# A gate in one step from PSUM, softmax sums spread in f16 halves, wider conversion and a new instruction order

## The chip, the cores and the metric

The kernel runs on one core of a Trainium2 chip. The metric is device time of one execution, in microseconds. In the text TensorE is the matmul engine (PE in the rows, PEld for its weight loads), VectorE is DVE, ScalarE is ACT, GpSimd is POOL, and SP is the engine that only issues transfers.

## What is computed

Attention for 4 batches of 12 heads (448 positions of 64), then a gated layer that mixes positions, then a feed-forward layer with a layer norm, all in f32 accuracy:

```python
q_n, k_n = rmsnorm(q, g_q), rmsnorm(k, g_k)
attn = softmax(q_n @ k_n.T / sqrt(64))              # sum + 1e-9 in the divisor
x = heads side by side of (attn @ v)                # 4 x 448 x 768
h = maximum(x @ w_in, 0)                            # 768 -> 1024
u, v = h[..., :512], h[..., 512:]
v_n = (v - mean(v)) / sqrt(var(v) + 1e-6)
v_s = einsum('ts,bsd->btd', w_spatial, v_n) + b_spatial[None, :, None]
x = (u * v_s) @ w_out                               # 512 -> 768
xn = layernorm(x) * g_ln
out = x + maximum(xn @ w_ch1, 0) @ w_ch2            # 768 -> 3072 -> 768
```

All weights but `w_spatial` come as 64-bit floats.

## The kernel before

f32 accuracy on f16 matmuls comes from splitting each operand into a high and a low f16 part and adding three products (high·high, high·low, low·high). Operands are scaled by powers of two first. `sum_scale` (L70) makes such a scale: VectorE casts partial maxima, TensorE adds them over the partitions by a product with ones (L83, tiles `ssb` and `pssc`), VectorE shifts exponents (L85 to L90, `sst`, `wsc`).

Attention goes in 24 pairs of heads. `att_slot` (L341) makes the scores of a pair in four groups (`s_mm`, L240, two score banks `ps_s`), their maximum (L251, VectorE), the exponential (L256, ScalarE), splits it into f16 halves (L275 ScalarE, L276 VectorE) and multiplies by v (L300; the first six pairs in f32, L293). `av_scale` (L304) spreads the reciprocals of the softmax sums, 7 per partition, over the positions: VectorE puts them on a diagonal `dg` (L311), TensorE multiplies it by a block of ones (L314, f32), ScalarE copies the result to `rb` (L316), which `av_out` multiplies in (L327).

The gated layer, `moe1` (L543), runs once per batch. It makes v and its norm (L563 to L577, `vn16`), u (L584, relu and scale on ScalarE at L587), then the spatial product for each of four quarters f of 128 columns (L597, tile `pss`, two banks). What follows it is:

```python
nc.vector.scalar_tensor_tensor(vs, ps[:, :S], isp[:, 0:1], c.bsp, op0=ALU.mult, op1=ALU.add)
nc.gpsimd.tensor_tensor(u[:, f], u[:, f], vs, op=ALU.mult)
nc.vector.tensor_reduce(gm[:, f:f + 1], u[:, f], axis=AX.X, op=ALU.max, apply_absolute_value=True)
```

and after the fourth quarter `sum_scale` over the four maxima, the f16 halves of the gated values (L611 ScalarE, L612 VectorE, `g16`) and the output product (L625, L635), which goes to DRAM (`x2d`). The layer of batches 0 to 2 lies beside attention, that of batch 3 beside the layer norms of the first half (batches 0 and 1).

`load_weight` (L395) turns 64-bit weights into f32 with three integer operations on VectorE per row block (L415 to L417). For the 12 blocks of `w_ch1` a transfer brings three row blocks of 256 columns each, for `w_ch2` one of 768.

The feed-forward layer runs in 12 blocks of 256 hidden columns and two halves of 896 positions: `ffn1` (L704, seven products of nine matmuls with sums between them on VectorE, L711 to L736, tiles `ps1x` to `ps1w` in three banks) and `ffn2` (L755, twelve matmuls per 128 positions, tile `ps2` with two buffers, added to the result by VectorE at L759). `prep_w1` and `prep_w2` load and split the weights of a block, `layernorm` (L645) makes the input.

The order on every engine is set at the end by `issue_order` (L1019): a planner runs forwards and backwards over the whole program with costs written in the code, and the table `SHAKES` says with which random shifts (seed, size, passes) the priorities are moved between runs. Every engine works through its queue in the order so found. SP's queue holds the transfers.

## Time and profile before

| | |
|---|---|
| time, median of 3 runs | 1175.62 us (1172.11 to 1179.37) |
| profiled execution, its own time | 1177.03 us |
| its span, first to last instruction | 1175.2 us |
| mean granted clock of TensorE | 0.967 |
| TensorE busy | 1049.7 us, 89% |
| VectorE busy | 958.4 us, 82% |
| ScalarE busy | 592.0 us, 50% |
| GpSimd busy | 295.6 us, 25% |

A profile is one execution. Busy time of an engine is the time in which at least one of its instructions ran. A row of a timeline has the start, the duration, the line of the kernel and the tile written and read; what stands in brackets is the idle time before it and what ended it. The chain of waits is followed back from the last instruction, at each step to what released it.

### The profile page before, as it was taken

The page shows a single profiled execution, that of the slowest core. Times are in us where ns is not written, and L with a number is a line of the kernel's source. Part 1 is how long each engine was busy: PE and PEld are TensorE (multiplying, and loading weights), DVE is VectorE, ACT ScalarE, POOL GpSimd, SP SyncE. Part 2 cuts the span into 40 slices and gives each one's busy share as a digit, 9 for nine tenths or more (in the row PEclk, how much of TensorE's full clock was granted, in tenths as well). Part 3 has the DMA queues.
Part 4 walks back from the last instruction along what each step waited for, and adds up shares of the span by engine and source line. Part 5 has one row for each costly group of instructions (what it writes and reads, how often), then busy time and mean ns, then how long its engine had stood idle before and what let it go on. Part 6 is the DMA issues. An engine that isn't in the chain of part 4 may idle for free.

```text
span 1175.2 us, 16716 instructions
## 1 busy us (share of the span) xinstructions
PE 1049.7 (89%) x6173; PEld 549.9 (47%) x6173; DVE 958.4 (82%) x1724; ACT 592.0 (50%) x1128; POOL 295.6 (25%) x209
## 2 busy tenths in 40 slices
PE   0679879989969998957789999999999999999998
PEld 0234324444435444423345555555555555555554
DVE  6798888869895987877988897888979788787755
ACT  2789878668776964646434334232423423243310
POOL 3454453726945520322001011010101101010100
PEclk9999879989989999978899999999999999999999
DMA  7978889899999996767773212112121211211013
GB/s 244 240 201 221 192 169 201 168 219 202 183 199 193 183 161 182 160 147 218 177 161 106 81 54 81 54 55 81 54 72 37 81 54 55 81 54 55 1 41 148
DMA packets 248913, 154.70 MB, mean 132 GB/s; under 512 B 209600, under 2 KB 226048, under 8 KB 248832
## 3 DMA queue, kind: packets, MB, share of 16 engines
q1 hardware_dynamic: 244448, 142.63, 51.4%
q10 hardware_dynamic: 4384, 11.01, 2.8%
q8 instruction: 48, 0.79, 0.3%
q14 instruction: 33, 0.27, 0.1%
HBM read 86.63 MB, written 11.01 MB: 83 GB/s over the span
## 4 chain that ended last, share of the span: by engine, by line
PE 48%; DVE 4%; issue 0%; DVEq 0%
PE ps L755 25%; PE ps1w L704 6%; PE ps1z L704 6%; PE ps1x L704 6%; PE ps1y L704 3%; DVE x L669 1%; DVE x L759 1%; DVE w1v L509 0%; DVE r_f L417 0%; DVE lst L656 0%; DVE r_f L416 0%; DVE h L717 0%; DVE lv L677 0%; DVE lv L679 0%; DVE lv L678 0%
## 5 line engine op out<-in xcount | busy, mean ns | idle before, releaser
L755 PE MATMUL ps<-w,h 128*128 128x384 f16 x2016 | 356.9, 327 | 7.8 <-DVE x L759 3.8
L755 PEld LDWEIGHTS <-h 128*128 128x128 f16 x2016 | 197.1, 98 | 150.7 <-issue 10.3
L759 DVE SCALAR_TENSOR_TENSOR x<-ps,wio,x 128x768 f32<-128x768 f32 x168 | 170.2, 1014 | 61.8 <-PE ps L755 60.3
L704 PEld LDWEIGHTS <-w1v 128*128 128x128 f16 x1512 | 147.7, 98 | 136.7 <-issue 8.9
L500 POOL TENSOR_TENSOR sums<-r_f 128x384 f32<-128x384 f32 x12 | 13.1, 1089 | 464.2 <-ACT r_f L497 464.2
L240 PE MATMUL ps_s<-hT 128*64 128x448 f16 x672 | 99.5, 386 | 32.6 <-ACT pexp L256 27.9
L256 ACT ACTIVATE pexp<-ps_s,nb 128x448 f32<-128x448 f32 x168 | 107.0, 650 | 33.1 <-DVE nb L251 32.1
L251 DVE TENSOR_REDUCE nb<-ps_s 128x2 f32<-128x896 f32 x96 | 91.2, 966 | 24.6 <-PE ps_s L240 24.1
L704 PE MATMUL ps1w<-xnT,w1v 128*128 128x448 f16 x432 | 92.7, 359 | 5.4 <-DVE rst_x L537 3.4
L704 PE MATMUL ps1x<-xnT,w1v 128*128 128x448 f16 x432 | 91.0, 352 | 0.0
L704 PE MATMUL ps1z<-xnT,w1v 128*128 128x448 f16 x432 | 90.6, 352 | 0.0
L276 DVE SCALAR_TENSOR_TENSOR p<-pexp,p 128x896 f16<-128x896 f32 x72 | 79.3, 1104 | 12.9 <-ACT p L275 12.7
L240 PEld LDWEIGHTS <-hT 128*64 128x64 f16 x672 | 39.8, 115 | 89.8 <-issue 56.9
L275 ACT ACTIVATE p<-pexp 128x896 f16<-128x896 f32 x72 | 61.6, 862 | 1.6 <-DMA pT<-p 0.7
L185 POOL TENSOR_TENSOR rs<-ss,mhalf 128x28 f32<-128x28 f32 (+1 forms) x12 | 58.4, 4868 | 13.1 <-DVE ss L182 8.5
L563 PE MATMUL psv<-w_v,xT 128*128 128x512 f16 (+1 forms) x360 | 61.2, 341 | 0.0
L584 PE MATMUL psu<-xT,w_u 128*128 128x448 f16 x288 | 59.8, 353 | 1.2 <-ACT vr L567 1.0
L203 POOL TENSOR_TENSOR qk<-raw,qk 128x896 f16<-128x896 f32 x23 | 45.5, 1979 | 55.8 <-ACT qk L202 54.0
L417 DVE SCALAR_TENSOR_TENSOR r_f<-r_w,r_f 128x256 int32<-128x256 int32 (+1 forms) x96 | 56.1, 584 | 1.3
L625 PE MATMUL pso<-w_o,g 128*128 128x384 f16 x288 | 53.0, 334 | 2.2 <-ACT g L611 1.9
L416 DVE SCALAR_TENSOR_TENSOR r_f<-r_w,r_f 128x256 int32<-128x256 int32 (+1 forms) x96 | 53.4, 556 | 1.5
L724 ACT ACTIVATE tp<-ps1x 128x448 f32<-128x448 f32 x24 | 13.0, 542 | 75.7 <-PE ps1x L704 75.4
(214 smaller groups left out, 1677.5 us busy)
## 6 DMA issues: line engine op xcount, KB each, us to landing
r_w<-in_moe_w_ch_dram SPq DMA_DIRECT2D x48, 768.0 KB, 4.4
raw<-in_q_dram SPq DMA_DIRECT2D x24, 224.0 KB, 3.4
raw<-in_k_dram SPq DMA_DIRECT2D x24, 224.0 KB, 3.5
vraw<-in_v_dram SPq DMA_DIRECT2D x24, 224.0 KB, 3.8
vpre<-in_v_dram SPq DMA_DIRECT2D x12, 448.0 KB, 4.6
...
```

Of the source, the lines that this page charges most:

```text
L185: nc.gpsimd.tensor_tensor(rs, ss, c.mhalf[:, 0:14 * m], op=ALU.pow)
L240: nc.tensor.matmul(ps[hd * 64:hd * 64 + 64, :S], p.hT[:, blk, hd * 64:hd * 64 + 64], kt[:, :, hd * 64:hd * 64 + 64], start=(t == 0), stop= ...
L251: nc.vector.tensor_reduce(nb[:, 0:n], ps[:, 0:n, :S], axis=AX.X, op=ALU.max, negate=True)
L256: nc.scalar.activation(pe[:, j, :], ps[:, j, :S], AF.Exp, bias=nb[:, j:j + 1], scale=1.0, accum_out=p.sm[:, blk:blk + 1])
L275: nc.scalar.activation(p16[:, 0:n, 0], x, AF.Copy, scale=2.0 ** 14)
L276: nc.vector.scalar_tensor_tensor(p16[:, 0:n, 1], x, 2.0 ** 14, p16[:, 0:n, 0], op0=ALU.mult, op1=ALU.subtract)
L417: nc.vector.scalar_tensor_tensor(o, lo, 29, o, op0=ALU.logical_shift_right, op1=ALU.bitwise_or)
L563: nc.tensor.matmul(ps[m * h:m * h + m, 0:hn], xT[:, k, x, t * P:t * P + m], wv[:, w, k, h * hn:(h + 1) * hn], start=(n == 0), stop=(n == l ...
L584: nc.tensor.matmul(ps[:, :S], wu[:, w, k, f * P:(f + 1) * P], xT[:, k, x, :], start=(n == 0), stop=(n == len(mms) - 1))
L704: nc.tensor.matmul(ps, w[:, a, x, d], xnT[:, :, 21 * y + 3 * b + d], start=first and n == 0, stop=n == 8, skip_group_check=True)
L755: nc.tensor.matmul(ps[:, e, 0:QK], h16[:, f, x, t * P:(t + 1) * P], w2[:, y, f, e * QK:(e + 1) * QK], start=n == 0, stop=n == 5)
L759: nc.vector.scalar_tensor_tensor(x2, ps[:, :, 0:QK], io[:, 0:1], x2, op0=ALU.mult, op1=ALU.add)
```

## The change

- *Gate.* A bound of |v_s| is made once, when `w_spatial` is loaded (`vbound2`). In `moe1` the maxima are taken of u alone, right behind its relu, and the scale comes from them and the bound, ahead of the spatial products. The bias enters the spatial product as three rows of bf16 (`bias3`) with one more matmul, the scale goes into `isp`. One VectorE step takes the product out of PSUM and multiplies it by u, ScalarE copies it to f16, VectorE makes the remainder. GpSimd's product, the tile `vs` and the broadcast of the bias to all partitions (`bsp`) go.
- *Softmax sums.* The reciprocals are split into two f16 halves (`s16`), the diagonal is f16 with 896 columns, and two f16 matmuls add up the halves. `rb` has a buffer of its own.
- *Conversion.* The three operations run over all row blocks of a transfer at once (768 columns).
- *Order.* `SHAKES` has 23 entries in place of 5.

```diff
--- before.py
+++ after.py
@@ -307,13 +307,18 @@
     p = c.pr[i]
     nc.vector.tensor_scalar(p.sm, p.sm, 1e-9, None, op0=ALU.add)
     nc.vector.reciprocal(p.sm, p.sm)
-    dg = c.att.tile([P, 64, NB], F32, tag="dg", name=f"dg{i}", bufs=1)
-    nc.vector.tensor_tensor(dg, p.sm[:].unsqueeze(1).to_broadcast([P, 64, NB]),
-                            c.eye2[:].unsqueeze(2).to_broadcast([P, 64, NB]), op=ALU.mult)
+    s16 = c.small.tile([P, 2, NB], F16, tag="s16", name=f"s16_{i}", bufs=2)
+    nc.vector.tensor_scalar(s16[:, 0], p.sm, 2.0 ** 15, None, op0=ALU.mult)
+    nc.vector.scalar_tensor_tensor(s16[:, 1], p.sm, 2.0 ** 15, s16[:, 0], op0=ALU.mult, op1=ALU.subtract)
+    dg = c.att.tile([P, 2, NB, 64], F16, tag="dg", name=f"dg{i}", bufs=1)
+    nc.vector.tensor_tensor(dg.rearrange("p t n q -> p (t n) q"),
+                            s16.rearrange("p t n -> p (t n)").unsqueeze(2).to_broadcast([P, 2 * NB, 64]),
+                            c.eye2[:].unsqueeze(1).to_broadcast([P, 2 * NB, 64]), op=ALU.mult)
     pr = c.ps_o.tile([P, 512], F32, tag="ps_o", name=f"ps_r{i}")
-    nc.tensor.matmul(pr[:, :S], c.head, dg.rearrange("p q n -> p (q n)"), start=True, stop=True)
-    p.rb = c.att.tile([P, S], F32, tag="dg", name=f"rb{i}", bufs=1)
-    nc.scalar.activation(p.rb, pr[:, :S], AF.Copy, scale=2.0 ** 14 if i in PE_PAIRS else 1.0)
+    for t in range(2):
+        nc.tensor.matmul(pr[:, :S], c.head, dg[:, t].rearrange("p n q -> p (n q)"), start=(t == 0), stop=(t == 1))
+    p.rb = c.att.tile([P, S], F32, tag="rb", name=f"rb{i}", bufs=1)
+    nc.scalar.activation(p.rb, pr[:, :S], AF.Copy, scale=2.0 ** -15 if i in PE_PAIRS else 2.0 ** -29)
 
 
 def av_out(c, i):
@@ -325,7 +330,7 @@
     xT = c.xT[b]
     x = c.att.tile([P, S], F32, tag="xo", name=f"xo{i}", bufs=1)
     nc.vector.tensor_tensor(x.rearrange("d (p n) -> d p n", n=NB), p.po[:, :S].rearrange("d (n p) -> d p n", n=NB),
-                            p.rb.rearrange("d (p n) -> d p n", n=NB), op=ALU.mult)
+                            p.rb.rearrange("d (n p) -> d p n", n=NB), op=ALU.mult)
     if i in PE_PAIRS:
         split(c, x, xT[:, hp, 0, :], xT[:, hp, 1, :], c.sv[b][:, 0:1])
     else:
@@ -410,11 +415,11 @@
         raw = c.wraw.tile([P, step, n, 2], I32, tag="wide", name=f"{name}_w{j}", bufs=c.wide_bufs)
         nc.sync.dma_start(out=raw.rearrange("p k n t -> p k (n t)"),
                           in_=src[j * P:(j + step) * P].bitcast(I32).rearrange("(k p) n -> p k n", p=P))
-        for i in range(step):
-            lo, hi, o = raw[:, i, :, 0], raw[:, i, :, 1], wi[:, j + i]
-            nc.vector.tensor_scalar(o, hi, 3, 0x3FFFFFF8, op0=ALU.logical_shift_left, op1=ALU.bitwise_and)
-            nc.vector.scalar_tensor_tensor(o, hi, -(1 << 30), o, op0=ALU.bitwise_and, op1=ALU.bitwise_or)
-            nc.vector.scalar_tensor_tensor(o, lo, 29, o, op0=ALU.logical_shift_right, op1=ALU.bitwise_or)
+        o = wi[:, j:j + step].rearrange("p k n -> p (k n)")
+        lo, hi = (raw.rearrange("p k n t -> p (k n) t")[:, :, t] for t in range(2))
+        nc.vector.tensor_scalar(o, hi, 3, 0x3FFFFFF8, op0=ALU.logical_shift_left, op1=ALU.bitwise_and)
+        nc.vector.scalar_tensor_tensor(o, hi, -(1 << 30), o, op0=ALU.bitwise_and, op1=ALU.bitwise_or)
+        nc.vector.scalar_tensor_tensor(o, lo, 29, o, op0=ALU.logical_shift_right, op1=ALU.bitwise_or)
     return w
 
 
@@ -459,6 +464,29 @@
         nc.sync.dma_start_transpose(out=spT[:, t], in_=sp16.rearrange("p a k -> p (a k)"))
         yield 1
     c.w["sp"] = (spT, sc)
+    bp = c.small.tile([P, NB], F32, tag="bp", name="bp", bufs=1)[:64]
+    nc.sync.dma_start(out=bp, in_=c.b_sp_d.rearrange("(p n) -> p n", n=NB))
+    bq = c.small.tile([P, NB], F32, tag="bq", name="bq", bufs=1)
+    nc.vector.memset(bq, 0.0)
+    nc.vector.tensor_tensor(bq[:64], bp, bp, op=ALU.mult)
+    vb = c.small.tile([P, 2], F32, tag="vb", name="vb", bufs=1)
+    nc.vector.tensor_reduce(vb[:, 1:2], bq, axis=AX.X, op=ALU.add)
+    nc.vector.tensor_reduce(vb[:, 0:1], mx, axis=AX.X, op=ALU.add)
+    nc.vector.scalar_tensor_tensor(vb[:, 0:1], vb[:, 0:1], float(S * DH), vb[:, 1:2], op0=ALU.mult, op1=ALU.add)
+    vb16 = c.small.tile([P, 1], BF16, tag="vb16", name="vb16", bufs=1)
+    nc.vector.tensor_scalar(vb16, vb[:, 0:1], 2.0, 2.0 ** -60, op0=ALU.mult, op1=ALU.max)
+    ps = c.ps_x.tile([P, 512], F32, tag="ps_x", name="ps_vb")
+    nc.tensor.matmul(ps[:, 0:1], c.ones, vb16, start=True, stop=True)
+    c.vbound2 = c.const.tile([P, 1], F32, name="vbound2")
+    nc.vector.tensor_copy(c.vbound2, ps[:, 0:1])
+    b16 = c.small.tile([P, 3, NB], BF16, tag="b16", name="b16", bufs=1)[:64]
+    nc.vector.tensor_scalar(bp, bp, sc[:64, 0:1], 2.0 ** 9, op0=ALU.mult, op1=ALU.mult)
+    c.bias3 = c.const.tile([3, S], BF16, name="bias3")
+    for j in range(3):
+        nc.vector.tensor_copy(b16[:, j], bp)
+        if j < 2:
+            nc.vector.tensor_tensor(bp, bp, b16[:, j], op=ALU.subtract)
+        nc.sync.dma_start(out=c.bias3[j:j + 1, :].rearrange("o (p n) -> o p n", n=NB), in_=b16[:, j])
 
 
 def moe1_weights(c):
@@ -577,6 +605,7 @@
         nc.vector.tensor_tensor(lo, vr[:m], vn16[:m, t, 0], op=ALU.subtract)
 
     u = c.m1.tile([P, NF, S], F32, tag="u", name=f"u{b}", bufs=1)
+    gm = c.small.tile([P, NF], F32, tag="gm", name=f"gm{b}")
     for f in range(NF):
         ps = c.ps_m.tile([P, 512], F32, tag="ps_m", name=f"psu{b}_{f}")
         mms = [(w, x, k) for w, x in ((0, 0), (0, 1), (1, 0)) for k in range(NC6)]
@@ -585,31 +614,27 @@
                              start=(n == 0), stop=(n == len(mms) - 1))
         yield len(mms) * MM448
         nc.scalar.activation(u[:, f], ps[:, :S], AF.Relu, scale=iu[:, 0:1])
-
+        nc.vector.tensor_reduce(gm[:, f:f + 1], u[:, f], axis=AX.X, op=ALU.max)
+    g2 = c.small.tile([P, NF], F32, tag="gm2", name=f"gm2_{b}")
+    nc.vector.tensor_tensor(g2, gm, gm, op=ALU.mult)
+    sg = sum_scale(c, g2, f"g{b}", c.vbound2[:, 0:1])
+    io = c.small.tile([P, 1], F32, tag="io", name=f"io{b}")
+    nc.vector.tensor_tensor(io, sg[:, 1:2], swo[:, 1:2], op=ALU.mult)
     isp = c.small.tile([P, 1], F32, tag="isp", name=f"isp{b}")
-    nc.vector.tensor_scalar(isp, ssp[:, 1:2], 2.0 ** -9, None, op0=ALU.mult)
-    gm = c.small.tile([P, NF], F32, tag="gm", name=f"gm{b}")
+    nc.vector.tensor_scalar(isp, ssp[:, 1:2], sg[:, 0:1], 2.0 ** -9, op0=ALU.mult, op1=ALU.mult)
+    g16 = c.m1.tile([P, NF, 2, S], F16, tag="g16", name=f"g16_{b}", bufs=1)
     for f in range(NF):
         ps = c.ps_m.tile([P, 512], F32, tag="ps_m", name=f"pss{b}_{f}")
         mms = [(x, w, k) for x, w in ((0, 0), (0, 1), (1, 0)) for k in range(NSC) if x == 0 or k < S // P]
         for n, (x, w, k) in enumerate(mms):
             m = P if k < S // P or w == 0 else S % P
             nc.tensor.matmul(ps[:, :S], vn16[:m, k, x, f * P:(f + 1) * P], spT[:m, :, w * NSC + k, :],
-                             start=(n == 0), stop=(n == len(mms) - 1))
-        yield len(mms) * MM448
-        vs = c.m1.tile([P, S], F32, tag="vs", name=f"vs{b}_{f}", bufs=2)
-        nc.vector.scalar_tensor_tensor(vs, ps[:, :S], isp[:, 0:1], c.bsp, op0=ALU.mult, op1=ALU.add)
-        nc.gpsimd.tensor_tensor(u[:, f], u[:, f], vs, op=ALU.mult)
-        nc.vector.tensor_reduce(gm[:, f:f + 1], u[:, f], axis=AX.X, op=ALU.max, apply_absolute_value=True)
-    g2 = c.small.tile([P, NF], F32, tag="gm2", name=f"gm2_{b}")
-    nc.vector.tensor_tensor(g2, gm, gm, op=ALU.mult)
-    sg = sum_scale(c, g2, f"g{b}")
-    io = c.small.tile([P, 1], F32, tag="io", name=f"io{b}")
-    nc.vector.tensor_tensor(io, sg[:, 1:2], swo[:, 1:2], op=ALU.mult)
-    g16 = c.m1.tile([P, NF, 2, S], F16, tag="g16", name=f"g16_{b}", bufs=1)
-    for f in range(NF):
-        nc.scalar.activation(g16[:, f, 0], u[:, f], AF.Copy, scale=sg[:, 0:1])
-        nc.vector.scalar_tensor_tensor(g16[:, f, 1], u[:, f], sg[:, 0:1], g16[:, f, 0], op0=ALU.mult, op1=ALU.subtract)
+                             start=(n == 0), stop=False)
+        nc.tensor.matmul(ps[:, :S], c.ones[0:3, :], c.bias3, start=False, stop=True)
+        yield (len(mms) + 1) * MM448
+        nc.vector.scalar_tensor_tensor(u[:, f], ps[:, :S], isp[:, 0:1], u[:, f], op0=ALU.mult, op1=ALU.mult)
+        nc.scalar.activation(g16[:, f, 0], u[:, f], AF.Copy)
+        nc.vector.tensor_tensor(g16[:, f, 1], u[:, f], g16[:, f, 0], op=ALU.subtract)
 
     t0 = b * S
     while t0 < (b + 1) * S:
@@ -787,7 +812,10 @@
 WINDOW = 3413
 
 
-SHAKES = ((0, 0, 4), (1003, 1000, 3), (1033, 20000, 2), (1069, 1000, 3), (1161, 20000, 1))
+SHAKES = ((0, 0, 2), (556, 3000, 2), (1748, 20000, 1), (1711, 1000, 3), (1453, 8000, 1), (1124, 20000, 1), (257, 300,
...
@@ -1074,12 +1103,12 @@
 
     c.ident = eye = c.wraw.tile([P, P], F32, tag="ident", name="ident", bufs=1)
     make_identity(nc, eye[:])
-    c.eye2 = c.const.tile([P, 64], F32, name="eye2")
+    c.eye2 = c.const.tile([P, 64], F16, name="eye2")
     nc.vector.tensor_tensor(c.eye2, eye[:, 0:64], eye[:, 64:P], op=ALU.add)
-    c.head = c.const.tile([P, P], F32, name="head")
+    c.head = c.const.tile([P, P], F16, name="head")
     nc.vector.memset(c.head, 0.0)
     for a in (0, 64):
-        nc.vector.memset(c.head[a:a + 64, a:a + 64], 2.0 ** -14)
+        nc.vector.memset(c.head[a:a + 64, a:a + 64], 1.0)
     warm = c.small.tile([P, 28], F32, tag="ss2", name="warm", bufs=2)
     nc.scalar.activation(warm, c.mhalf, AF.Exp)
     att_load(c, 0)
@@ -1104,8 +1133,6 @@
     nc.tensor.matmul(ps[:, 0:1], c.ones, gb, start=True, stop=True)
     c.gmax2 = c.const.tile([P, 1], F32, name="gmax2")
     nc.vector.tensor_copy(c.gmax2, ps[:, 0:1])
-    c.bsp = c.const.tile([P, S], F32, name="bsp")
-    nc.sync.dma_start(out=c.bsp, in_=b_spatial.partition_broadcast(P))
     n = B * NPAIR
 
     def att(lo, hi):
```

The new order moves nearly every instruction; two places are shown, rows as they stand in an engine's queue.

The first is VectorE's queue at the end of batch 3's gate. Before, its rows there were, from the layer norm's remainder (`x16`) on, with `r2_0_f` the first block of `w_ch2` in conversion, `gm3` the maxima of quarters 2 and 3, and `lmv`, `rst` layer norm:

```order
L669 TENSOR_TENSOR x16_0_2_3_1_5342<-lv0_2_5304,x16_0_2_3_0_5339 112x1536
L537 TENSOR_SCALAR rst_x0_3_0_5392<-lmv0_3_0_5388 112x1
L537 TENSOR_SCALAR rst_x0_3_1_5404<-lmv0_3_1_5400 112x1
L415 TENSOR_SCALAR r2_0_f_5787<-r2_0_w1_5793 128x768
L603 TENSOR_REDUCE gm3_5449<-u3_5284 128x1
L659 TENSOR_SCALAR lmv0_3_0_5388<-lmv0_3_0_5388,rsr_x0_3_0_5394 112x1
L416 SCALAR_TENSOR_TENSOR r2_0_f_5787<-r2_0_w1_5793,r2_0_f_5787 128x768
L659 TENSOR_SCALAR lmv0_3_1_5400<-lmv0_3_1_5400,rsr_x0_3_1_5406 112x1
L417 SCALAR_TENSOR_TENSOR r2_0_f_5787<-r2_0_w1_5793,r2_0_f_5787 128x768
L603 TENSOR_REDUCE gm3_5449<-u3_5284 128x1
L669 TENSOR_TENSOR x16_0_3_0_1_5413<-lv0_3_5385,x16_0_3_0_0_5410 112x1152
L605 TENSOR_TENSOR gm2_3_5535<-gm3_5449 128x4
```

And now, with `u3` the step from PSUM of quarters 2 and 3 (line 635 of the changed kernel), `g16` the remainder (637), 421 and 422 the conversion, 694 and 702 layer norm:

```order
L635 SCALAR_TENSOR_TENSOR u3_5380<-pss3_2_5600,isp3_5565,u3_5380 128x448
L523 TENSOR_SCALAR wgs_0_5121<-gln_219,wsc_1_0_5118 128x6
L421 SCALAR_TENSOR_TENSOR r2_0_f_5879<-r2_0_w1_5885,r2_0_f_5879 128x768
L694 TENSOR_TENSOR x16_0_3_0_1_5512<-lv0_3_5484,x16_0_3_0_0_5509 112x1152
L637 TENSOR_TENSOR g16_3_5567<-u3_5380,g16_3_5567 128x448
L635 SCALAR_TENSOR_TENSOR u3_5380<-pss3_3_5627,isp3_5565,u3_5380 128x448
L422 SCALAR_TENSOR_TENSOR r2_0_f_5879<-r2_0_w1_5885,r2_0_f_5879 128x768
L702 TENSOR_TENSOR lv0_3_5484<-lv0_3_5484 112x384
L637 TENSOR_TENSOR g16_3_5567<-u3_5380,g16_3_5567 128x448
L622 TENSOR_TENSOR io3_5563<-wsc_g3_5560,wsc_o_1423 128x1
```

The two maxima have gone from this place (they stand ahead of the spatial products), and each quarter's step and remainder follow each other with at most four rows between them.

The second is TensorE's queue in the feed-forward part, at block 5's output for positions 1408 to 1535 (`ps2_5_11`). Before, a group of nine (`ps1x`, line 704) and one of twelve (`ps2`, line 755) stood whole, one behind the other; this is where one changes to the other:

```order
L704 LDWEIGHTS w1v6_8343
L704 MATMUL ps1x_6_0_8649<-xnT0_4966,w1v6_8343 128x448
L755 LDWEIGHTS h16_5_1_8436
L755 MATMUL ps2_5_11_8740<-w2_5_7937,h16_5_1_8436 128x384
L755 LDWEIGHTS h16_5_1_8436
```

And now (729 is `ffn1`, 780 is `ffn2`; `ps2_5_10` and `ps2_5_11` are two output banks):

```order
L729 LDWEIGHTS w1v6_8375
L729 MATMUL ps1z_6_0_8697<-xnT0_5074,w1v6_8375 128x448
L780 LDWEIGHTS h16_5_1_8456
L780 MATMUL ps2_5_10_8731<-w2_5_7969,h16_5_1_8456 128x384
L729 LDWEIGHTS w1v6_8375
L729 MATMUL ps1z_6_0_8697<-xnT0_5074,w1v6_8375 128x448
L780 LDWEIGHTS h16_5_1_8456
L780 MATMUL ps2_5_10_8731<-w2_5_7969,h16_5_1_8456 128x384
L780 LDWEIGHTS h16_5_1_8456
L780 MATMUL ps2_5_11_8760<-w2_5_7969,h16_5_1_8456 128x384
L780 LDWEIGHTS h16_5_1_8456
L780 MATMUL ps2_5_10_8731<-w2_5_7969,h16_5_1_8456 128x384
```

The groups are mixed matmul by matmul, and the first matmul on an output bank stands nearer to the last one on its use before.

## Rows read from the trace of the kernel before

**Rows 1.** Busy time by stretch: us, then each engine, granted clock, DMA share, GB/s.
```profile
50.00:500.00 450.00, 400.48 (x2464) 189.12 (x2464) 380.61 (x642) 342.02 (x698) 212.32 (x138) 0.95 0.90 190
250.00:300.00 50.00, 48.74 (x334) 24.22 (x333) 36.24 (x63) 37.59 (x76) 25.73 (x18) 1.00 0.89 203
300.00:350.00 50.00, 39.98 (x258) 19.15 (x255) 47.52 (x68) 40.07 (x86) 34.21 (x17) 0.94 1.01 194
501.30:604.60 103.30, 72.58 (x385) 37.62 (x385) 90.55 (x194) 48.92 (x68) 15.89 (x17) 0.85 0.72 171
605.00:1150.00 545.00, 544.45 (x3142) 305.68 (x3141) 439.09 (x782) 177.32 (x320) 47.41 (x40) 1.00 0.20 65
```

**Rows 2.** Chain of waits around its switch: start us, us, engine, tile, line.
```profile
603.65 0.94 DVE x L759
604.63 2.11 PE ps L755 x12
...
665.10 1.95 PE ps L755 x12
667.05 1.70 PE ps1z L704 x9
```

**Rows 3.** TensorE's waits up to 605 us: total us, times, longest.
```profile
PE ps_s L240 <- ACT pexp L256: 27.9, 22, 4.0
```

**Rows 4.** Timeline of TensorE, 490 to 605 us: start, us, row, idle before it.
```profile
494.21 7.03 PE L597 MATMUL pss<-w_sp,vn 128*128 128x448 f16 x33 [0.37 <-ACT u L587]
511.17 0.25 PE L83 MATMUL pssc_g<-ssb_g,ones 128*128 128x1 bf16 x4 [9.93 <-DVE ssb_g L80]
513.93 0.53 PE L635 MATMUL pso<-w_o,g 128*64 128x384 f16 x2 [2.51 <-ACT g L611]
...
595.84 4.06 PE L755 MATMUL ps<-w,h 128*128 128x384 f16 x24 [1.83 <-DVE x L759]
```

**Rows 5.** Timeline of VectorE in the same stretch.
```profile
507.88 0.60 DVE L603 TENSOR_REDUCE gm<-u 128x1 f32<-128x448 f32 x1
...
593.51 1.35 DVE L669 TENSOR_TENSOR x<-lv,x 112x1152 f16<-112x1152 f32 x1
594.78 1.01 DVE L759 SCALAR_TENSOR_TENSOR x<-ps,wio,x 128x768 f32<-128x768 f32 x1
```

**Rows 6.** VectorE by line and shape: busy us, mean ns | idle before.
```profile
L416 DVE SCALAR_TENSOR_TENSOR r_f<-r_w,r_f 128x256 int32<-128x256 int32 x72 | 30.3, 421 | 1.2
...
L200 DVE TENSOR_TENSOR raw<-raw,rs 128x896 f32<-128x896 f32 x24 | 26.8, 1123 | 1.1 <-POOL rs L189 1.1
...
L416 DVE SCALAR_TENSOR_TENSOR r_f<-r_w,r_f 128x768 int32<-128x768 int32 x24 | 23.1, 963 | 0.3
...
L311 DVE TENSOR_TENSOR dg<-sm,eye 128x448 f32<-128x448 f32 x24 | 19.2, 800 | 0.1
...
L308 DVE TENSOR_SCALAR sm<-sm 128x7 f32<-128x7 f32 x24 | 5.5, 231 | 2.5 <-ACT pexp L256 2.5
```

**Rows 7.** TensorE by line and shape.
```profile
L314 PE MATMUL ps_r<-dg,head 128*128 128x448 f32 x48 | 25.5, 615 | 0.3 <-DVE dg L311 0.2
```

**Rows 8.** Timeline of VectorE, 330 to 352 us.
```profile
332.15 1.71 DVE L333 TENSOR_TENSOR xT<-xo,xT 128x448 f16<-128x448 f32 x1
...
335.92 1.91 DVE L276 SCALAR_TENSOR_TENSOR p<-pexp,p 128x896 f16<-128x896 f32 x1
...
341.34 0.61 DVE L311 TENSOR_TENSOR dg<-sm,eye 128x448 f32<-128x448 f32 x1
```

**Rows 9.** Timeline of GpSimd in the same stretch.
```profile
331.00 2.38 POOL L203 TENSOR_TENSOR qk<-raw,qk 128x896 f16<-128x896 f32 x1 [1.75 <-DMA pT<-p]
333.35 3.53 POOL L602 TENSOR_TENSOR u<-u,vs 128x448 f32<-128x448 f32 x2
```

**Rows 10.** GpSimd by line.
```profile
L602 POOL TENSOR_TENSOR u<-u,vs 128x448 f32<-128x448 f32 x16 | 22.2, 1396 | 23.5 <-DVE vs L601 21.9 <-DVE sm L308 1.6
```

**Rows 11.** Timeline of TensorE, 330 to 352 us.
```profile
340.31 2.48 PE L240 MATMUL ps_s<-hT 128*64 128x448 f16 x12 [3.96 <-ACT pexp L256]
```

More of the change, by code (lines that the diff above doesn't have):

```diff
@@ L109, in att_setup @@
     nc = c.nc
-    gk = c.att.tile([P, S], F32, tag="dg", name="gk", bufs=1)[:, 0:D]
+    gk = c.att.tile([P, S], F32, tag="rb", name="gk", bufs=1)[:, 0:D]
     gg = c.const.tile([P, D], F32, tag="gg", name="gg")
@@ L1045 @@
     c.w_in_d, c.w_sp_d, c.w_out_d, c.w1_d, c.w2_d = w_in, w_spatial, w_out, w_ch1, w_ch2
+    c.b_sp_d = b_spatial
     c.out = out.rearrange("b s e -> (b s) e")
```

3 rows, old and new, of the table SHAKES are left out of this document.

## The prediction

> **What bounds the kernel now.** I read the busy table by stretch first, then the chain of waits, then the waiting times of TensorE, and last the timelines at the places found. From 605 us on TensorE is busy 544.45 of 545 us at full clock [rows 1]: nothing that leaves its matmuls as they are can shorten that part, only lengthen it. The chain of waits says the same: up to 604.6 us it lies on VectorE, from 604.63 us on it is matmuls behind matmuls, 12 of the 384-column kind in 1.95 us and 9 of the 448-column kind in 1.70 us, which is 0.163 and 0.189 us each [rows 2]. So the time is the moment of that switch plus a fixed tail, and a change pays only before 604.6 us.
>
> Ahead of the switch there are two stages. From 50 to 500 us (attention, with the first three batches of the gated layer) TensorE is busy 400.5 of 450 us and VectorE 380.6; they take turns, TensorE full in 250 to 300 us and VectorE in 300 to 350 us [rows 1]. TensorE's largest wait up to 605 us is 27.9 us for the exponentials that free its score banks, in 22 waits [rows 3]; one of them, 3.96 us, is at 340.31 us [rows 11]. From 501.3 to 604.6 us (last batch, layer norm, first feed-forward blocks) VectorE is busy 90.6 of 103.3 us, TensorE 72.6 at a mean granted clock of 0.85, so in part at the lower of its two levels [rows 1]. Its largest hole there is the end of the last gate: the spatial products end at about 501.2 us, then 9.93 us go by until the scale sums and 2.51 us more until the output product [rows 4]. The last column maximum on which the sums rest starts only at 507.88 us, behind weight conversion and layer norm [rows 5].
>
> **The change part by part.** All is summed against the profiled execution's own time, 1177.0 us (span 1175.2 and 1.8 around it); the median of the three runs is 1.4 us under it.
>
> *Gate.* The scale now comes from a bound that needs only the relu half, so the four products, the step from PSUM, the f16 copy and the remainder follow each other with no sum in between. The sum is still there: TensorE runs its four small products behind the second spatial product, and the third one needs the bank that the first step frees. That chain (sums, shifts, one step) is like the one that took 2.51 us [rows 4], with some layer norm rows standing among it in the new VectorE order; I take 4 us. After the last spatial product one step and one copy come before the output product can go on: 1.5 us, worked out from 0.61 us for a 448-column operation [rows 8] on each of two engines and the way between them. 5.5 us in place of 12.4: **−7 us**, bounds −12 (no wait left) and 0 (the wait only moves). VectorE keeps three 448-column operations per quarter. The bias row adds 16 products of 448 columns, 16 × 0.189 = 3.0 us of TensorE.
>
> *Softmax sums on TensorE.* The f32 spread takes 48 matmuls, 25.5 us [rows 7], 1.06 us per pair; two f16 products take 0.38 us. 24 × 0.68 = 16.3 us less; with the bias row 13.3 us less. That counts where TensorE is the fuller engine. As the two take turns between 50 and 500 us, I take half: **−6.5 us**, bounds −13 and 0.
>
> *Softmax sums on VectorE.* The diagonal grows from 448 to 896 columns, and two operations on 7 columns come in front. The nearest row of 896 columns with two inputs takes 1.12 us, the present diagonal 0.80, a 7-column one 0.23 [rows 6]: +0.32 + 0.46 = +0.78 us. Neighbours overlap by about 0.08 us (the row at 593.51 us ends at 594.86, the next starts at 594.78 [rows 5]), which makes it 0.62 us, 24 × 0.62 = 15 us. The lower bound is a diagonal as cheap as 448 columns, free at 0.61 us [rows 8]: +0.11 us, 2.6 us in all. [...] Half of it lies where VectorE is the fuller: **+7.5 us**, bounds +1 and +15. [...]
>
> *The product on GpSimd goes.* It is 16 × 1.40 = 22.2 us [rows 10]. Beside GpSimd VectorE's two-input rows stretch: at 332.15 us 1.71 us for 448 columns that take 0.61 when free, at 335.92 us 1.91 for 896 that take about 1.1 [rows 6, 8], 1.9 us lost beside GpSimd rows of 2.38 and 3.53 us [rows 9]. A third of 22.2 is 7 us, half of it on the path: **−3.5 us**, bounds −7 and 0. The wait at 340.31 us [rows 11] comes behind just such a stretch.
>
> *Wider conversion.* Three 256-column operations of 0.421 us become one of 768 columns, 0.963 [rows 6]: −0.30 us, for each of two two-input operations, twice per block: −1.2 us per block. Two and a half blocks stand ahead of the switch, where VectorE is nearly full: **−3 us**. The other nine and a half lie under the full TensorE and give nothing; they would cost nothing either.
>
> *Bias load.* The broadcast of 224 KB goes and four transfers of under 2 KB come. The first is read by VectorE at its very start, ahead of the chain for the gain rows, which itself has waited for transfers issued just before it; the other three are read hundreds of microseconds later: 0.
>
> *Order.* No row prices it, so it is bounded. In the first stage it can at best take away the 27.9 us for the exponentials [rows 3], at worst add some; I take a quarter, **−7 us**. In the feed-forward part it can only lose. Between the last matmul on an output bank and the first on its next use stood 30 matmuls (18 × 0.189 + 12 × 0.163 = 5.35 us), the median of 132 such places; now the median is 2.2 us, the least 7 matmuls (1.32 us), and 52 of 132 places are under 2.0. The bank comes free when VectorE's 1.01 us update is done; at 594.78 us it started behind a 1.35 us layer norm row, and TensorE waited 1.83 us [rows 4, 5]. With VectorE free, 1.32 us suffices; with an operation in front it does not. I take **+3 us**, bounds 0 and 31 (52 × 0.6).
>
> Sum: −7 − 6.5 + 7.5 − 3.5 − 3 − 7 + 3 = −16.5 us; 1177.0 − 16.5 = 1160.5, less the 1.4 to the median 1159: I say **1160 us**, with the switch at about 586 us.
>
> **The rivals.**
> 1. *The order gives more*: 20 us of the 27.9 go in place of 7. For it: these are waits on what stands where in three queues, which is what an order sets. Against: the scores still go through two buffers. 1160 − 13 = 1147 us.
> 2. *VectorE decides attention*: its +15 us come in full, TensorE's saving, GpSimd's and the order's nothing. For it: 300 to 350 us, 47.5 of 50 us busy [rows 1]. Against: 250 to 300 us. 1177 − 7 + 15 − 3 = 1182 us.
> 3. *The gate's wait only moves* (the change doesn't do there what it says): the small products in the middle of the spatial ones hold TensorE as long as the sums did behind them. For it: the bank of the third product hangs on that chain. Against: the maxima now wait for no spatial product. 1167 us.
> 4. *Slower: the feed-forward part stalls.* Each of the 52 tight places loses 0.6 us, two thirds of an operation in front: 31 in place of 3 us, 1160 + 28 = 1188 us. It decides from 0.53 us per place. For it: a full TensorE has no slack to give, and the wait at 595.84 us [rows 4]. Against: VectorE is busy 439 of 545 us there [rows 1], and 11 us less after the wider conversion.
>
> **How the numbers follow.** Forecast 0.48, rivals 0.12, 0.15, 0.13 and 0.12 in turn. A measurement of this kernel tells a change from none at about 1%, under 1163.9 or over 1187.4 us. Faster: 0.43 of the forecast's 0.48 (its own range is 1151 to 1168 us) and all of rival 1, 0.55. Slower: 0.10 of rival 4 and 0.02 of rival 2, 0.12. The rest, 0.33, is the same. The range runs from rival 1, a little lower, to rival 2: 1145 to 1181 us, which leaves out some 0.1 on each side.
>
> **What would show it.** Right: the wait for the scale sums under 2 us in the last batch and some 4 us at the third spatial product; the spread at 9 to 11 us for 48 matmuls; the diagonal at 1.1 us or a little over; conversion rows of 768 columns only; the chain's switch between 580 and 592 us; TensorE without more than 5 us of idle time behind it. Wrong: idle time of TensorE behind output-bank updates all through the feed-forward part (rival 4); VectorE fuller than 90% between 50 and 500 us with TensorE emptier (rival 2); a wait of over 8 us at the gate's third product (rival 3). The forecast is wrong as a whole if the switch does not move.

## The result and the profile after

The changed kernel takes 1161.28 us (median of four executions, 1159.11 to 1165.11), the kernel before 1174.63 beside it: a ratio of 0.9885, 95% interval 0.9844 to 0.9927. That is 13.3 us less, and 1.3 us above the number forecast. The profiled execution has a span of 1163.3 us against 1175.2, 11.9 us less, and all comparisons of rows below are against these two.

In the chain of waits (start us, us, engine, tile, line) the switch from VectorE to TensorE has moved from 604.63 [rows 2] to 591.21 us; L780 and L729 are the lines of `ffn2` and `ffn1` in the changed kernel:

```profile
587.56 1.00 DVE x L784
588.56 1.67 DVE x L694
591.21 1.30 PE ps L780 x7
593.08 1.51 PE ps1x L729 x8
```

Where the time went is read at the same pieces of work, not at fixed times: by 500 us after has the scale sums of its last gate behind it, before has not. I take the end of TensorE's last matmul for u (line 584, 613 in after), the end of the last gate's output product (625, 650) and the switch. The rows of its timeline that end there, before, then after:

```profile
492.33 0.35 PE L584 MATMUL psu<-xT,w_u 128*128 128x448 f16 x1
...
528.69 7.64 PE L625 MATMUL pso<-w_o,g 128*128 128x384 f16 x46
```

```profile
474.40 7.92 PE L613 MATMUL psu<-xT,w_u 128*128 128x448 f16 x41
...
521.32 0.98 PE L650 MATMUL pso<-w_o,g 128*128 128x384 f16 x5
```

The stretches between them, before, then after (columns as in [rows 1]; TensorE's busy time is the first figure after the length):

```profile
0.00:492.68 492.68, 403.50 (x2485) 191.08 (x2485) 408.71 (x723) 359.01 (x728) 226.04 (x147) 0.95 0.89 195
492.68:536.33 43.65, 30.84 (x172) 15.22 (x171) 35.31 (x81) 18.28 (x30) 13.14 (x12) 0.84 0.67 155
536.33:604.63 68.30, 49.93 (x253) 25.76 (x252) 62.71 (x127) 36.24 (x51) 9.00 (x10) 0.88 0.78 183
604.63:1175.20 570.57, 565.41 (x3266) 317.86 (x3265) 451.70 (x795) 178.47 (x322) 47.41 (x40) 1.00 0.21 69
```

```profile
0.00:482.32 482.32, 399.94 (x2492) 184.55 (x2493) 426.73 (x765) 355.39 (x723) 206.28 (x135) 0.96 0.92 197
482.32:522.30 39.98, 33.54 (x170) 14.93 (x169) 34.01 (x64) 19.52 (x32) 8.20 (x6) 0.87 0.77 181
522.30:591.21 68.91, 51.90 (x264) 26.38 (x263) 66.12 (x133) 37.85 (x51) 11.27 (x12) 0.88 0.78 179
591.21:1163.30 572.09, 566.35 (x3266) 317.53 (x3265) 432.26 (x682) 174.55 (x322) 43.79 (x40) 1.00 0.21 70
```

| stretch, us | before | after | | TensorE idle before | after |
|---|---|---|---|---|---|
| up to the last product of u | 492.7 | 482.3 | −10.4 | 89.2 | 82.4 |
| from there to the end of the gate | 43.7 | 40.0 | −3.7 | 12.8 | 6.4 |
| from there to the switch | 68.3 | 68.9 | +0.6 | 18.4 | 17.0 |
| behind the switch | 570.6 | 572.1 | +1.5 | 5.2 | 5.7 |

**Most of the gain, 10.4 of 11.9 us, is there before the last gate makes its spatial products.** In this stretch TensorE's idle time fell by 6.8 us and its busy time by 3.6. Before had done six spatial products (1.3 us) more by its end, so that some 9 us are left for the same work. The last gate gave 3.7 us, or 5.0 with these six on its side, and what stands behind it gave back 2.1. Read between fixed times, the same traces mislead: from 50 to 500 us TensorE is idle 49.5 us in before and 49.3 in after, as if nothing had been gained there, because the gate's waits lie on this side of 500 us in after and on the other side in before.

What TensorE waits for between 50 and 500 us in after (total us, times, longest):

```profile
PE ps_s L240 <- ACT pexp L256: 20.3, 17, 3.8
PE pss L631 <- DVE u L635: 7.4, 5, 3.4
PE ps_r L319 <- DVE dg L314: 4.4, 5, 1.5
PE ps_r L319 <- DVE xo L332: 4.4, 5, 1.6
```

The wait for the exponentials fell by 7.6 us (from 27.9 up to 605 us, [rows 3]). New are 8.8 us at the spread of the softmax sums, for the diagonal and for attention's output product, which must release the bank, and 7.4 us at the gate's spatial products, 3.4 of them in the last gate.

At the end of the last gate the timeline of TensorE shows the scale sums in the middle of the spatial products, with no wait ahead of them; the third product waits 3.38 us and the output product 0.17 and 1.32, 4.9 us in place of 12.4 [rows 4]:

```profile
485.68 2.46 PE L631 MATMUL pss<-w_sp,vn 128*128 128x448 f16 x11
...
488.37 0.25 PE L83 MATMUL pssc_g<-ssb_g,ones 128*128 128x1 bf16 x4
492.00 4.49 PE L631 MATMUL pss<-w_sp,vn 128*128 128x448 f16 x11 [3.38 <-DVE u L635]
...
496.90 4.01 PE L631 MATMUL pss<-w_sp,vn 128*128 128x448 f16 x11
...
501.98 0.65 PE L650 MATMUL pso<-w_o,g 128*128 128x384 f16 x3 [0.17 <-DVE u L635]
...
505.43 0.35 PE L660 MATMUL pso<-w_o,g 128*64 128x384 f16 x2 [1.32 <-DVE g L637]
```

That is 7.5 us less of waiting for 3.7 to 5.0 us of time. The granted clock is 1.00 ahead of the 3.38 us wait (485.6 to 488.2 us) and 0.55 in the mean behind it (491.9 to 501.2 us; 0.50 up to 500 us), and eleven products take 4.49 and 4.01 us where they took 2.46 ahead of it. Before has such a stretch too, but TensorE stands still in most of it (0.50 from 504 to 513.5 us, 0.25 us busy). In both traces the granted clock is 1.00 or 0.50 at every moment. The bias rows add 1.6 us.

The rows by line that answer to [rows 6, 7] (busy us, mean ns | idle before):

```profile
L422 DVE SCALAR_TENSOR_TENSOR r_f<-r_w,r_f 128x768 int32<-128x768 int32 x48 | 47.4, 987 | 0.5
...
L200 DVE TENSOR_TENSOR raw<-raw,rs 128x896 f32<-128x896 f32 x24 | 34.5, 1442 | 0.1
L314 DVE TENSOR_TENSOR dg<-s,eye 128x896 f16<-128x896 f16 x24 | 29.9, 1247 | 0.2
...
L332 DVE TENSOR_TENSOR xo<-ps_o,rb 128x448 f32<-128x448 f32 x24 | 22.2, 926 | 10.1 <-PE ps_o L300 9.9
...
L311 DVE TENSOR_SCALAR s<-sm 128x7 f16<-128x7 f32 x24 | 8.3, 348 | 0.1
...
L312 DVE SCALAR_TENSOR_TENSOR s<-sm,s 128x7 f16<-128x7 f32 x24 | 3.7, 156 | 0.2
```

```profile
L319 PE MATMUL ps_r<-dg,head 128*128 128x448 f16 x48 | 15.2, 388 | 8.9 <-DVE dg L314 4.4 <-DVE xo L332 4.4
```

The softmax sums cost VectorE 28.8 us more: the diagonal 29.9 against 19.2, the two new small operations 12.0, the sum's own small one 1.5 less (5.5 to 4.0), and attention's output product 22.2 against 14.6. The last I had not priced: it now reads the spread sums with a step of 64 elements. TensorE's spread saves 10.3 us (25.5 to 15.2).

### The profile page after: what moved, and what is told of

The parts are those of the page before. It is cut to its first block, busy times and chain, and to the rows that moved or that the text cites. A ratio compares the mean times of both kernels' runs of the same rounds, so it can differ in the third digit from the quotient of the medians.

```text
span 1163.3 us, 16645 instructions
## 1 busy us (share of the span) xinstructions
PE 1051.7 (90%) x6190; PEld 543.4 (47%) x6190; DVE 959.1 (82%) x1641; ACT 587.3 (50%) x1128; POOL 269.5 (23%) x193
## 4 chain that ended last, share of the span: by engine, by line
PE 45%; DVE 8%; DMA 1%; ACT 1%; issue 1%; POOL 0%; DVEq 0%; ACTq 0%
PE ps L780 24%; PE ps1w L729 6%; PE ps1z L729 6%; PE ps1x L729 6%; PE ps1y L729 3%; DVE x L784 2%; DVE w1v L537 1%; DVE x L694 1%; DMA r_w<-in_moe_w_ch_dram 1%; DVE h L742 1%; DVE lst L681 0%; ACT r_f L525 0%; DVE r_f L422 0%; DVE r_f L421 0%; POOL rsr_x L567 0%
## 5 line engine op out<-in xcount | busy, mean ns | idle before, releaser
L780 PE MATMUL ps<-w,h 128*128 128x384 f16 x2016 | 385.9, 329 | 13.2 <-ACT w L396 5.1
L780 PEld LDWEIGHTS <-h 128*128 128x128 f16 x2016 | 197.2, 98 | 164.4 <-issue 15.1
L729 PEld LDWEIGHTS <-w1v 128*128 128x128 f16 x1512 | 147.0, 98 | 127.4 <-issue 3.7
L240 PE MATMUL ps_s<-hT 128*64 128x448 f16 x672 | 104.4, 392 | 26.1 <-ACT pexp L256 20.3
L528 POOL TENSOR_TENSOR sums<-r_f 128x384 f32<-128x384 f32 x12 | 12.1, 1011 | 457.7 <-ACT r_f L525 457.7
L729 PE MATMUL ps1x<-xnT,w1v 128*128 128x448 f16 x432 | 108.4, 352 | 0.2 <-DVE tc L736 0.2
L729 PE MATMUL ps1z<-xnT,w1v 128*128 128x448 f16 x432 | 106.3, 352 | 0.0
L729 PE MATMUL ps1w<-xnT,w1v 128*128 128x448 f16 x432 | 105.2, 352 | 1.0 <-DVE tu L736 0.9
L276 DVE SCALAR_TENSOR_TENSOR p<-pexp,p 128x896 f16<-128x896 f32 x72 | 72.7, 1014 | 4.6 <-ACT p L275 4.1
L741 ACT ACTIVATE h<-td 128x448 f16<-128x448 f32 x24 | 13.8, 574 | 93.1 <-DVE td L736 93.1
L631 PE MATMUL pss<-w_sp,vn 128*128 128x448 f16 (+1 forms) x176 | 46.7, 381 | 8.8 <-DVE u L635 7.4
L729 PE MATMUL ps1y<-xnT,w1v 128*128 128x448 f16 x216 | 53.0, 352 | 0.9 <-DMA xnT<-x 0.9
```

The costliest lines, as they stand in the source:

```text
L240: nc.tensor.matmul(ps[hd * 64:hd * 64 + 64, :S], p.hT[:, blk, hd * 64:hd * 64 + 64], kt[:, :, hd * 64:hd * 64 + 64], start=(t == 0), stop= ...
L276: nc.vector.scalar_tensor_tensor(p16[:, 0:n, 1], x, 2.0 ** 14, p16[:, 0:n, 0], op0=ALU.mult, op1=ALU.subtract)
L729: nc.tensor.matmul(ps, w[:, a, x, d], xnT[:, :, 21 * y + 3 * b + d], start=first and n == 0, stop=n == 8, skip_group_check=True)
L780: nc.tensor.matmul(ps[:, e, 0:QK], h16[:, f, x, t * P:(t + 1) * P], w2[:, y, f, e * QK:(e + 1) * QK], start=n == 0, stop=n == 5)
```

## The experiments

The forecast was a sum over edits and an order. Theory A: the edits bring the gain, each about what its rows say, and any order planned for them serves. Theory B: the new order brings it, and the edits cancel each other. To tell them apart most runs below *keep an order*: the planner is replaced by a list in which every instruction that two kernels have in common stands where it stood, and a new one right behind what it depends on, in the planner's own reckoning. All of them compute the whole result.

| run | time, us | ratio to before (95%) |
|---|---|---|
| after | 1161.3 | 0.9885 (0.9844 to 0.9927) |
| all edits, before's order kept | 1208.2 | 1.0274 (1.0242 to 1.0306) |
| gate alone, before's order kept | 1192.2 | 1.0131 (1.0104 to 1.0159) |
| softmax sums alone, before's order kept | 1201.0 | 1.0207 (1.0162 to 1.0252) |
| conversion alone, before's order kept | 1177.6 | 1.0018 (1.0002 to 1.0035) |
| all edits, planned with before's table | 1176.9 | 1.0011 (0.9993 to 1.0028) |
| no edit, planned with after's table | 1181.0 | 1.0035 (1.0011 to 1.0059) |
| no edit, a 19-entry table of its own | 1180.4 | 1.0022 (1.0006 to 1.0039) |
| gate and conversion, a 14-entry table of their own | 1182.8 | 1.0044 (1.0029 to 1.0060) |
| after, softmax sums undone, order kept | 1161.1 | 0.9889 (0.9859 to 0.9919) |
| after, sums read as they lie, same order | 1160.1 | 0.9871 (0.9847 to 0.9895) |
| after, conversion undone, order kept | 1176.3 | 1.0000 (0.9977 to 1.0023) |
| after, gate undone, order kept | 1198.3 | 1.0182 (1.0156 to 1.0209) |

**All edits in the order of before.** The code is that of after; only the order changes (`PLAN` is the list of places):

```diff
+    place = array.array("H", zlib.decompress(base64.b85decode("".join(PLAN))))
...
-    for l in schedule(g, prio)[1].values():
+    rows = {}
+    for o in sorted(g.ops, key=lambda o: place[o.n]):
+        rows.setdefault(o.eng, []).append(o)
+    for l in rows.values():
         for a, b in zip(l, l[1:]):
             tc.add_manual_dep(b.i, a.i.name, link, reason="order")
```

> All three edits (gate, softmax sums, wider conversion) in the kernel before's own instruction order: every instruction that both kernels have stands where it stood, the new ones right behind what they depend on. Theory A (the edits bring the gain, and most of it at the last gate): 1163 to 1169 us, that is 6 to 12 us under before, with the switch of the chain to TensorE at 593 to 599 us. Theory B (the new order brings the gain, the edits cancel each other): 1172 to 1178 us, no difference from before.

1208.2 us, 33 us *over* before: neither theory. The single edits say which of them lose there.

**The gate alone in the order of before** (the gate's part of the diff, `bias3` and `vbound2` with it).

> Only the gate is changed, in the kernel before's order. By my sum -7 -3.5 (GpSimd's product gone) and a little for the bias row: about -9 us, 1166 us; by the theory that the gate's wait only moves: within 3 us of before. The wait for the scale sums (9.93 us) should be under 2 us; at the third spatial product of the last batch a wait of about 4 us should stand.

1192.2 us, 17 us over before. The waits that I had priced fell (2.2 us ahead of the last scale sums, a little over the 2 expected, and 0.7 in place of 4 at the third product), but another took their place. TensorE's timeline, then ScalarE's:

```profile
508.29 0.24 PE L83 MATMUL pssc_g<-ssb_g,ones 128*128 128x1 bf16 x4 [2.24 <-DVE ssb_g L80]
510.53 4.49 PE L626 MATMUL pss<-w_sp,vn 128*128 128x448 f16 x11 [0.69 <-DVE u L630]
...
535.11 4.00 PE L645 MATMUL pso<-w_o,g 128*128 128x384 f16 x12 [9.29 <-ACT x2o L658]
```

```profile
533.11 1.48 ACT L691 ACTIVATE x<-lv 112x1536 f16<-112x1536 f32 x1 [4.76 <-DVE lv L700]
534.49 0.56 ACT L658 ACTIVATE x2o<-pso,io 128x384 f32<-128x384 f32 x1
```

The output product needs its bank back from the copy `x2o`. In the old order that copy stands behind a layer norm row, which itself waits for VectorE. In before this row ran at 515.46 us, when the output product had just begun (513.93), and the copy then waited for TensorE; here the row runs at 533.11 us, and TensorE waits 9.29 us for the copy. Ahead of the gate 10 us are lost as well: the last product of u ends at 502.9 us in place of 492.7. The new VectorE rows wait there in the middle of its queue, 8.0 us between 50 and 500 us (for u, for the spatial product and for the f16 copy); that this is the cause is argued, not shown. So in this order the rows behind the gate eat its saving.

**The softmax sums alone in the order of before** (`av_scale` and the layout that `av_out` reads; the diagonal and the spread sums share a buffer, as before).

> Only the softmax sums are changed, in the kernel before's order. By my prediction's terms TensorE -6.5 and VectorE +7.5: about +1 us, bounds -12 and +15. The trace of after shows one cost that I had not priced, the output product of attention at 0.93 us in place of 0.61 (24 times, 7.6 us of VectorE): with it theory A says +4 to +9 us, 1179 to 1184 us. A rival, that TensorE decides attention, says -5 to -12 us.

1201.0 us, 25 us over before, where 4 to 9 were expected: VectorE was busy 394.7 us of 450 (380.6 before), TensorE 379.1 (400.5). After has a buffer of its own for the spread sums; what the shared one costs here is not parted from the order.

**The conversion alone in the order of before** (three wide operations where nine stood).

> Only the conversion is widened, in the kernel before's order. The rows of after make it 24 us less of VectorE in all, 2.0 us per block; 2.5 blocks stand ahead of the switch. By my term -3 us, by the rows of after -5 us, if VectorE decides there; 0 if the wider operation only delays what stands behind it. Expected 1170 to 1176 us.

1177.6 us, no gain; 22 us less of VectorE (143.7 to 121.9 for the conversion) are worth nothing there.

**All edits, planned anew with before's table; and no edit, planned with after's.** Only the table changes:

```diff
-SHAKES = ((0, 0, 2), (556, 3000, 2), (1748, 20000, 1), ...
+SHAKES = ((0, 0, 4), (1003, 1000, 3), (1033, 20000, 2), (1069, 1000, 3), (1161, 20000, 1))
```

> All three edits, and the planner makes a new order for them, but with the kernel before's table of 5 entries. Theory A (any order planned for the edits lets them pay): 1158 to 1170 us. Theory B (the gain is that of the table found for this code): 1175 us or more; in the kept order the edits cost 33 us.

> The code of before, planned with the new table of 23 entries. Theory B, in its strong form (the table is better whatever the code): 1160 to 1168 us. Weak form (a table fits the code for which it was found): 1178 us or more, since before's own table was fitted to it.

1176.9 and 1181.0 us. An order planned for the edits makes up their 33 us, but no more; and the new table does nothing for the old code. Neither half has the gain.

**Longer tables for other code.** Two tables were found as the expectation says, one for the code of before, one for gate and conversion without the softmax sums.

> The code of before with none of the edits, planned with a table of 19 entries that was found for this code by trying entries and keeping those by which the planner's own end came earlier. Theory B1 (what counts is a long table found for the code at hand; the edits do nothing): 1158 to 1166 us, as after. Theory B2 (the edits take waits away that no order can, above all the scale sums of the last gate, and an order is needed to cash them): 1168 to 1176 us, and the wait for the scale sums at the last gate stays at 8 us or more.

> Gate and wider conversion, the softmax sums as before (f32, with the buffer of their own), planned with a table of 14 entries found for this code in the same way. Since the sums' edit was worth nothing in after's order (1161.1 against 1161.3 us), theory B2 expects 1156 to 1166 us, as after. If the sums' edit is needed after all: 1168 us or more.

1180.4 and 1182.8 us. The first rules B1 out, but it is also 4 us above B2's range. The wait at before's last gate remains, though 5.0 us ahead of the sums, not 8, with 5.5 behind them (between 480 and 560 us):

```profile
PE pso L635 <- ACT g L611: 5.5, 1, 5.5
PE pssc_g L83 <- DVE rst_x L537: 5.0, 1, 5.0
```

The second speaks against B2, by which it should have stood beside after. Tables kept by the planner's own reckoning gave nothing on the chip, for either code.

**After with the softmax sums undone, its order kept.**

```diff
-    dg = c.att.tile([P, 2, NB, 64], F16, tag="dg", name=f"dg{i}", bufs=1)
+    dg = c.att.tile([P, 64, NB], F32, tag="dg", name=f"dg{i}", bufs=1)
...
-    for t in range(2):
-        nc.tensor.matmul(pr[:, :S], c.head, dg[:, t].rearrange("p n q -> p (n q)"), start=(t == 0), stop=(t == 1))
+    nc.tensor.matmul(pr[:, :S], c.head, dg.rearrange("p q n -> p (q n)"), start=True, stop=True)
```

> The changed kernel in its own order, with the softmax sums as before (f32 diagonal of 448 columns, f32 spread, no split of the sums, sums read as they lie); the buffer of their own stays. TensorE has 10 us more by the rows (15.2 to 25.5), VectorE about 30 us less (diagonal 24 x 0.46, two small operations 24 x 0.5, output product 24 x 0.32). Theory A (VectorE decides attention): faster than after, 1150 to 1158 us. Rival (TensorE decides there, the edit pays in the new order): 1164 to 1172 us. In the old order the edit cost 25 us; if that was the edit itself and not its place in the order, this run is over 10 us under after.

1161.1 us, the time of after. Between 50 and 500 us VectorE has 20.4 us less to do than in after and TensorE 7.4 more, and TensorE's idle time falls by just that (after, then this run; the last gate's waits lie in this stretch in both):

```profile
50.00:500.00 450.00, 400.68 (x2467) 182.46 (x2467) 406.52 (x706) 341.47 (x694) 189.03 (x122) 0.94 0.92 192
50.00:500.00 450.00, 408.05 (x2477) 185.47 (x2476) 386.09 (x659) 343.14 (x697) 186.03 (x123) 0.95 0.93 193
```

Both theories of the expectation fall: the engines take turns there, and the edit moves work from one to the other at no gain.

**After with the sums read as they lie** (the order is the same instruction for instruction).

```diff
-    dg = c.att.tile([P, 2, NB, 64], F16, tag="dg", name=f"dg{i}", bufs=1)
+    dg = c.att.tile([P, 2, 64, NB], F16, tag="dg", name=f"dg{i}", bufs=1)
...
-                            p.rb.rearrange("d (n p) -> d p n", n=NB), op=ALU.mult)
+                            p.rb.rearrange("d (p n) -> d p n", n=NB), op=ALU.mult)
```

> The changed kernel in its own order, every instruction in its place; only the layout of the diagonal is position-major, so that the spread sums are read in the order in which they lie. Theory A (the step from 0.61 to 0.93 us of attention's output product comes from reading the sums with a stride, and VectorE decides attention): that row is back at 0.61 us, 7.6 us less of VectorE, the time 3 to 8 us under after, 1153 to 1158 us. Rival (the step has another cause, as GpSimd beside it): the row stays at 0.93 us and the time at 1161. Rival (the diagonal pays for it, since its inner run is now 7 long): the diagonal goes from 1.08 to over 1.2 us and the time does not move.

1160.1 us (1157.6 to 1160.8), the fastest of all, though its interval does not part it from after. The row is back, and the diagonal as before:

```profile
L314 DVE TENSOR_TENSOR dg<-s,eye 128x896 f16<-128x896 f16 x24 | 30.0, 1248 | 0.2
...
L332 DVE TENSOR_TENSOR xo<-ps_o,rb 128x448 f32<-128x448 f32 x24 | 14.7, 613 | 9.9 <-PE ps_o L300 9.9
```

The cause of the dearer row is shown. Its 7.5 us of VectorE are worth about 1 us, within the noise, where 3 to 8 were expected: that VectorE decides attention is not borne out.

**After with the conversion undone, its order kept.** The first of nine operations stands where the first wide one did, the others, block by block, from where the second stood.

> The changed kernel in its own order, with the conversion in operations of 256 columns, three where one stood. VectorE has 24 us more by the rows, about a fifth of it ahead of the switch. By my term +3 us, 1164 us; by the run of the conversion alone in the old order, where it gave nothing: within 2 us of 1161.

1176.3 us: the whole gain is gone, the largest surprise here. TensorE's waits behind 605 us, and its busy time there (after, then this run):

```profile
PE ps L780 <- DVE x L784: 9.1, 14, 1.3
PE ps1w L729 <- DVE tu L736: 1.2, 3, 0.6
PE ps1x L729 <- DVE tc L736: 1.1, 2, 0.9
```

```profile
605.00:1150.00 545.00, 543.77 (x3140) 305.23 (x3139) 418.21 (x663) 171.08 (x316) 43.79 (x40) 1.00 0.18 62
605.00:1150.00 545.00, 532.89 (x3056) 296.74 (x3055) 427.48 (x772) 171.43 (x316) 43.72 (x40) 1.00 0.19 61
```

In this profiled execution (1185.3 us, the longest of its ten) TensorE is 12.1 us idle where after has 1.2. Another 6.9 us are lost ahead of that, by the end of the gate's output product (529.2 us for 522.3). One of the fourteen places, on VectorE and then on TensorE:

```profile
736.24 0.43 DVE L422 SCALAR_TENSOR_TENSOR r_f<-r_w,r_f 128x256 int32<-128x256 int32 x1
736.58 1.94 DVE L784 SCALAR_TENSOR_TENSOR x<-ps,wio,x 128x768 f32<-128x768 f32 x2
```

```profile
737.65 2.27 PE L780 MATMUL ps<-w,h 128*128 128x384 f16 x13 [0.90 <-DVE x L784]
```

The update that frees the output bank starts when the last narrow conversion is through, and TensorE waits for it. So it is at four of the fourteen places; at six more the narrow conversion stands two or three rows ahead of the update, and three such waits are in after too. This is my rival 4, with its mechanism and its place; in this order the wide conversion keeps most of it away. Whether the longer work of the narrow rows does it or where the added ones stand is not parted, and how the 15 us of the median divide is not known, for the execution profiled is 9 us above it.

**After with the gate undone, its order kept** (one buffer for `vs` in place of two, for want of room).

> The changed kernel in its own order, with the gate of before: step from PSUM with the bias, GpSimd's product, maxima of the products, sums behind the last one, two halves; these rows stand right behind what they depend on, everything else keeps its place. By my term for the gate and GpSimd's product +10.5 us less 3 for the bias row, 1166 to 1172 us; by the theory that the gate is where the whole gain lies: 1172 to 1180 us; the wait for the scale sums of the last batch is back at 5 us or more.

1198.3 us, more than either theory. The scale sums wait four times, 22.3 us, once 15.2:

```profile
PE pssc_g L83 <- DVE ssb_g L80: 22.3, 4, 15.2
```

The order of after leaves no place for that chain, as the order of before left none for the new one. The run shows the price of an edit in an order made for another, not the worth of the gate.

## Why the prediction was right, and where it was not

The number, the range, the sign and the likeliest case held: 1161.3 for 1160, the switch at 591.2 in "580 to 592". On the profiled executions, for which the sum was made, it is further off: −16.5 us forecast, −11.9 measured, with after's the slowest of its four. Step by step it is less good still, and the sum closed in part by luck, because errors cancelled.

*Gate, −7.* Right for the waits that it was worked out from: 12.4 us became 4.9, with 3.4 at the third product where I said 4. The scale sums themselves wait no more. But the stretch got only 3.7 to 5.0 us shorter: behind the wait that is left the third and fourth product ran at a mean granted clock of 0.55 and took 4.49 and 4.01 us for eleven matmuls, not 2.46, and the bias rows cost 5.9 us of TensorE in all, not 3.0. What I left out besides is that the gain had to be collected: in the old order a copy behind a layer norm row took 9.3 us of it.

*Softmax sums, −6.5 and +7.5.* The net, +1, is what the run in the same order measures, 0 within its noise; that is luck, for both halves were wrong. I priced the spread at the pace of matmuls in a row, 0.189 us each; in pairs that wait for their diagonal they take 15.2 us for 48, not 9 to 11. VectorE pays 28.8 us, not 15. The diagonal itself held: 1.08 us in the middle of the 24, 1.07 the least, as the nearest row said. No run shows the +7.5 by itself: it is half of the 15 us, and that the diagonal would cost these and not the 2.6 of its lower bound was my estimate, which no row of before shows; the 24 of after took 1.07 to 2.77 us. Missed were the output product's new step, which stands in the diff (0.93 us for 0.61), and the small operations held up beside GpSimd (up to 1.63 us for 0.16).

*GpSimd's product, −3.5.* No run shows it by itself. GpSimd was busy 26 us less, and the f16 remainders of 896 columns went from 1.21 to 1.12 us in the mean, but the products of q and k (`raw`) went from 1.12 to 1.44 us in the mean [rows 6]: in the new order six of the 24, each beside a GpSimd row, took 1.6 to 4.4 us, against 1.08 for the middle one.

*Conversion, −3 ahead of the switch and nothing behind it.* The step that failed most plainly. It is larger than I priced, 24 us of VectorE and not 14 (12 blocks of 1.2), since I left out the one-input operation. In the old order it gave nothing; in the new one undoing it costs 13 to 15 us (ratio 1.0000 against 0.9885), and in the execution profiled 11 us of idle time appear *behind* the switch. I had called those blocks covered by a full TensorE, and in the next paragraph counted 52 places at which this same TensorE now depends on VectorE being free in time. The two paragraphs belonged together.

*Order, −7 and +3.* The exponentials gave the 7 us, though 8.8 came back at the spread and 4.0 at the spatial products of the first three gates. Up to the last product of u my terms for sums, GpSimd and order made −9.5 us, with some of the conversion's −3 besides; the traces show −10.4, or some −9 for the same work. As a sum that came out near, and two more executions in after's order, those with the sums undone and with the sums read as they lie, show no less (479.5 and 477.4 us there, before 492.7). No run parts it into my terms; the sums' edit gave none of it. Behind the switch 1.5 us were lost, inside +3. As a whole the order was sized too small: with the same edits it is the difference between 1176.9 and 1161.3 us, 16 us, not 4; and the edits in a newly planned order with before's table are worth nothing, where my terms for them made −12.5.

So theory A falls and B in its strong form as well. What the runs show is that edits and order act together: the new table without edits +4 to +6 us (and a long table of the old code's own +3), edits without this order +1 to +33, both together −13. The profiles show where after's table pays: with the same edits before's table ends the last product of u at 489.8 us (after 482.3), the gate at 528.1 (522.3), and needs 648.7 us from there (641.0). Gate and conversion with their own table are at the gate's end first of all, at 518.8 us, and then need 663.2. What is *not* settled: which rows of after's table do it. The planner's own reckoning is no guide to it (two tables that were better by it gave nothing), and whether the code of before would reach 1161 us with a table picked by its times on the chip was not tried; so it is not shown that the edits are needed at all.
